# Seven products for a unit pair of the first MLP layer in chunks 3 to 6, and four operand transposes moved into the attention stage

## The chip, the cores and the metric

The kernel runs on one core of a Trainium2 chip. The metric is the device time of one execution in microseconds (us). All times below are us unless marked ns. TensorE (PE) multiplies matrices, VectorE (DVE) and ScalarE (ACT) do elementwise work, GpSimd (POOL) masks, scales and issues loads, SyncE (SP) issues loads and stores. Each engine works through its own queue in order.

## The reference

Forgetting attention, and behind it a two-layer MLP with a tanh gelu. Inputs are float32.

```python
scores = scale * np.matmul(q, k.transpose(0, 1, 3, 2))      # 8 batches, 8 heads, 576 tokens, head size 64
cum = np.cumsum(np.log(np.clip(f, 0.0001, 1.0)), axis=-1)
scores = np.where(causal, -1000000000.0, scores + cum[:, :, :, None] - cum[:, :, None, :])
attn = softmax(scores)                                      # over the keys
x = np.matmul(attn, v).transpose(0, 2, 1, 3).reshape(4608, 512)
out = gelu_tanh(x @ w_in) @ w_out                           # 512 -> 2048 -> 512
```

## The kernel before

The MLP works on chunks of 512 tokens (nine, numbered 0 to 8), the attention on groups of four heads of one batch (sixteen "quads"). xT holds x transposed, in four blocks of 128 features. A stage of the steady part has two halves: the MLP's first layer of chunk c, and then attention for two quads, with the second layer of chunk c woven into it as filler for TensorE. The order is written out by hand: TABLES[c] is a string of words, which play(c) turns into instructions; every engine gets its instructions in the order of the words. FRONT does the same for chunks 0 and 1. The words that matter here:

- Y and X load ScalarE's table for gelu and exp. O.512 puts out what is left of the last chunk's second layer. F.n and f.n put out n steps of this chunk's.
- P.k is a plain unit of the first layer (mlp_in, L369, L376): eight matmuls for 256 of the 2048 hidden features, and one gelu. With a third number, P.k.1, it takes its PSUM tile from the pool psO ("po", one buffer, otherwise used by the attention products) and not from psS ("s", two buffers, otherwise used by the scores).
- R.k, said three times, does the units k and k + 4 together by seven products of half the size in place of eight (seven_in, L417, L423, L428, L432). Product one goes to bank pa, two to pb (both in psS), three to pc and four to pd (both in psM, "m", two buffers, otherwise the banks of the second layer), product five to pa again; the second R puts one more on pc and the third one on pd. VectorE makes six operations of it: a copy of pa, and adds from PSUM, three of which fill output tiles (h_st, in the pool ostage, three buffers, otherwise the tiles of the output stores). They are 28 matmuls of 256 columns against 16 of 512.
- R needs sums of weights, K.k.n (w_sums, L405: four operations on VectorE; they overwrite a part of w_in, so P.k and P.k+4 can't be used after them, and store three sums in an old chunk's part of xT, HOMES), and sums of x, T (x_sums, L390: four operations on VectorE for chunk c + 1, stored in chunk c's part of xT).
- G makes the sums that the second layer's own seven products need (gelu_sums, L483 to L489).
- TK.i and TQ.i transpose the loaded k and q of a quad on VectorE (L193), LK.i and LQ.i load those of a quad (L187, GpSimd's queue), LV loads v of a batch (L164, SP's queue). Buffers of k and q alternate between even and odd quads.
- S.i.r are scores and exp (L256, L264), M.i.r masks on GpSimd (L270, called selects below), D.i the denominators (L343 to L347), V.i.x an attention product and its xT product on VectorE (L355), VW.i the scaled v on GpSimd (L210, "vw product"), CL.i a small copy on VectorE (L215) that waits for VW.i.
- The second layer's output adds (L529) are VectorE's, its stores (L517) SP's. Its two banks are freed by the last output adds.

In stage c, the quads are q2 = 2c + 2, q3 = 2c + 3, q4 = 2c + 4. Before the change, R is used in chunks 7 and 8 alone. Chunks 2 to 6 are eight P each, with all of TK, TQ, LK and LQ for the next two quads near the start of the MLP half. K.1.0 to K.1.2 stand in the MLP of chunk 3, K.3.0 to K.3.2 in that of chunk 4, and K.1.3, K.3.3 and T at the end of stage 6.

Of the kernel before, what the change touches and what calls it, by code (L numbers as in the profile page):

```python
# [16 lines left out]
def kernel(  # L17
# [53 lines left out]
    """  # L71

    FRONT = """
        TQ.0 B.2.256 TK.1 SB TR LP.2@LQ.0 B.2.128 CW S.0.0 B.5.384 B.1.256 Z TQ.1 vw.0.0 S.0.2 WI.0 LQ.2 M.0.0 B.3.384 H.1.0.1
        LP.3 B.1.256 vw.1.0 WI.1@LU.4 W H.1.1.1 WI.3 B.2.256 WI.2 H.1.0.0 M.1.0.1 D.0.0 M.1.0.0 H.0.1.1 V.0.0.0 H.0.1.0 B.2.256 M.0.1 H.1.1.0 V.0.1.0
        D.1.0 H.0.3.0 B.2.128 V.1.0.0 LX.1.1 H.0.3.1 V.1.1.0 m.0.3.2 H.1.3.0 m.0.3.4 B.1.256 VW.1.1 H.1.3.1 B.4.128 vw.0.1 D.0.1 M.1.3 S.1.2 M.1.1 LK.2
        V.0.1.1 V.0.0.1 WO.0 J.0.1 D.1.1 J.0.0 WO.1@LV.1.1 V.1.1.1 V.1.0.1 J.0.3 WO.2@WI.1 VW.3 J.1.0 WO.3 LK.3 LQ.3 J.1.1 TQ.2 J.1.3 LQ.4
        LX.1.0@WO.2 TK.2 J.0.2 J.1.2 X LK.4 F.0.6 TK.3 B.3.256 S.2.0 LK.5 F.0.9 S.2.2 F.0.10 S.2.1 TQ.3 TQ.4 F.0.10 LV.2.0@LK.5 m.2.1 vw.2
        TK.4 S.3.0 f.0.1 M.2.2 CL.2 LQ.5 M.2.0 D.2 f.0.6 S.3.1 m.3.0 F.0.6 V.2.0 S.3.2 TK.5 LK.6 M.3.2 f.0.7 V.2.1 CL.3
        S.4.1 m.3.1 LQ.6 F.0.6 TQ.5 H.4.2.1 D.3 H.4.0.1 LQ.7 VW.4 H.4.0.0 V.3.1 v.3.0 f.0.3 H.4.2.0 CL.4 I.1.0 m.4.1 U.0 LV.2.1@LQ.5 I.1.4  # L80
        TQ.6 m.4.2.3 I.1.1 I.1.5 U.1 LV.3.0@LQ.7 m.4.2.2 TK.6 G.0 M.4.0 I.1.2 I.1.3 U.3 I.1.6 I.1.7 G.1.1.2 U.2 X F.1.14 S.5.0 f.1.28 S.5.1 D.4 M.5.0 f.1.16
# [2 lines left out]
    """

    HOMES = {1: 0, 3: 1}
    TABLES = {}
    TABLES.update(dict.fromkeys((2, 5), """
        Y O.512 P.0 P.1 TK.q3 TQ.q3 LK.q5 LQ.q5 TK.q4 TQ.q4 LK.q6 LQ.q6 LV P.4 P.5 G.0 P.2 P.3 P.6 P.7 G.1.1.2 X F.10 S.q3.0
        D.q2 M.q3.0 f.22 S.q3.1 V.q2.0 M.q3.1 VW.q3 f.18 S.q3.2 V.q2.1 M.q3.2 CL.q3 f.16 S.q4.0 D.q3 M.q4.0 f.18 S.q4.1 V.q3.0  # L90
        M.q4.1 VW.q4 f.9 V.q3.1 f.7 S.q4.2 M.q4.2 CL.q4
    """))
    TABLES.update(dict.fromkeys((3,), """
        Y O.512 P.0 P.1 TK.q3 TQ.q3 LK.q5 LQ.q5 TK.q4 TQ.q4 LK.q6 LQ.q6 LV K.1.0 K.1.1 K.1.2 P.4 P.5 G.0 P.2 P.3 P.6 P.7 G.1.1.2
        X F.10 S.q3.0 D.q2 M.q3.0 f.22 S.q3.1 V.q2.0 M.q3.1 VW.q3 f.18 S.q3.2 V.q2.1 M.q3.2 CL.q3 f.16 S.q4.0 D.q3 M.q4.0 f.18
        S.q4.1 V.q3.0 M.q4.1 VW.q4 f.9 V.q3.1 f.7 S.q4.2 M.q4.2 CL.q4
    """))
    TABLES.update(dict.fromkeys((4,), """
        Y O.512 P.0 P.1 TK.q3 TQ.q3 LK.q5 LQ.q5 TK.q4 TQ.q4 LK.q6 LQ.q6 LV K.3.0 K.3.1 K.3.2 P.4 P.5 G.0 P.2 P.3 P.6 P.7 G.1.1.2
        X F.10 S.q3.0 D.q2 M.q3.0 f.22 S.q3.1 V.q2.0 M.q3.1 VW.q3 f.18 S.q3.2 V.q2.1 M.q3.2 CL.q3 f.16 S.q4.0 D.q3 M.q4.0 f.18  # L100
        S.q4.1 V.q3.0 M.q4.1 VW.q4 f.9 V.q3.1 f.7 S.q4.2 M.q4.2 CL.q4
    """))
    TABLES.update(dict.fromkeys((6,), """
        Y O.512 P.0 P.1 TK.q3 TQ.q3 LK.q5 LQ.q5 LV P.4 P.5 G.0 P.2 P.3 P.6 P.7 G.1.1.2 X F.10 S.q3.0 D.q2 M.q3.0 f.22 S.q3.1
        V.q2.0 M.q3.1 VW.q3 f.18 S.q3.2 V.q2.1 M.q3.2 CL.q3 f.16 D.q3 f.18 V.q3.0 v.q3.1 T K.1.3 K.3.3 f.18
    """))
    TABLES.update(dict.fromkeys((7,), """
        Y O.512 P.0.1 R.1 P.4.1 R.1 R.1 R.3 P.2.1 R.3 G.0.1.2 P.6 R.3 G.0.3.4 G.1.1.2 T
    """))
    TABLES.update(dict.fromkeys((8,), """  # L110
        O.512 P.0.1 R.1 P.4.1 R.1 R.1 R.3 P.2.1 R.3 G.0.1.2 P.6 R.3 G.0.3.4 G.1.1.2
    """))

    singles = ctx.enter_context(tc.tile_pool(name="singles", bufs=1))
    ostage_pool = ctx.enter_context(tc.tile_pool(name="ostage", bufs=3))
# [664 lines left out]
```

## Time and profile before

| | |
|---|---|
| median of three runs | 330.25 us (330.21 to 332.17) |
| profiled execution, span from first to last instruction | 328.4 us |
| around it (median less span) | 1.85 us |
| granted TensorE clock | 1.000 of full speed |
| matmul L369 (plain units of the first layer) | 448, 99.0 us busy |
| matmul L504 (second layer by seven products) | some 2100 in three groups, 94 us busy |
| VectorE transposes L193 | 32, 39.9 us busy |

The page does not list the profiled execution's own device time apart from its span; the 1.85 us between the span and the median is taken as what lies around it. A row of the timeline has: start, duration, engine, line, operation, output and inputs, shapes, count, and in brackets the idle time before it with what ended it. Rows of the chain of waits have start, duration and the work. TensorE is busy 96% of the span; that share counts matmuls that overlap in the pipeline, so the chain of waits is what tells whether it is at its bound.

### The profile page before, as it was taken

Reading aid. Unit: us, or ns where it says so; the run is one execution under the profiler, and the core shown is the slowest. Engines: PE = TensorE matmul, PEld = TensorE weight load, DVE = VectorE, ACT = ScalarE, POOL = GpSimd, SP = SyncE. Lnnn points to the kernel's source line nnn. Section 1 sums busy time; section 2 is a strip of 40 time slices with the busy share of each in tenths; the row PEclk is TensorE's granted clock in tenths of the full one; section 3 lists DMA queues with packets and bytes.
Section 4 is the critical chain, followed back from the end, with each engine's and each line's share of the span. In section 5 each row is a group of like instructions: output and inputs, shape, how many; then the busy total and the mean of one; then the engine's idle time right before and its main releaser. Section 6 shows DMA issues by size and latency. Waiting matters only on the chain.

```text
span 328.4 us, 11961 instructions
## 1 busy us (share of the span) xinstructions
PE 316.9 (96%) x5421; PEld 206.5 (63%) x5421; DVE 206.4 (63%) x323; ACT 201.7 (61%) x231; POOL 110.6 (34%) x155
## 2 busy tenths in 40 slices
PE   3999999999999999999999999999999999999995
PEld 1458844545776477646774577557754777787684
DVE  4686039884887865674567456636553767875772
ACT  4685576866767586668656775768675841721630
POOL 8985572510504415520544054303440140000000
PEclk9999999999999999999999999999999999999999
DMA  7999999861124990295129711761110102002012
GB/s 123 210 214 215 168 230 199 167 165 24 36 40 94 236 208 31 94 187 108 37 68 182 140 37 36 160 122 36 36 66 0 36 21 81 2 32 98 0 35 96
DMA packets 44323, 33.42 MB, mean 102 GB/s; under 512 B 27488, under 2 KB 37856, under 8 KB 44272
## 3 DMA queue, kind: packets, MB, share of 16 engines
q0 software_dynamic: 8848, 16.58, 28.0%
q1 hardware_dynamic: 35280, 16.01, 18.4%
q8 instruction: 42, 0.69, 0.9%
q14 instruction: 9, 0.07, 0.1%
q10 hardware_dynamic: 144, 0.07, 0.1%
HBM read 36.85 MB, written 9.44 MB: 141 GB/s over the span
## 4 chain that ended last, share of the span: by engine, by line
PE 86%; DMA 3%; DVE 3%; ACT 3%; POOL 2%; issue 2%; POOLq 0%; DVEq 0%; ACTq 0%
PE ps_h L369 29%; PE ps_w L504 25%; PE po L324 9%; PE ps_s L256 8%; PE pso L574 4%; PE ps_h L458 4%; DMA v_nat<-in_v_dram 2%; PE ps_cd L417 2%; ACT pt L264 2%; PE ps_ab L417 2%; PE po_m L310 1%; POOL vw L210 1%; DMA out_dram<-o_st 1%; POOL v_nat L164 0%; PE ps_o L324 0%
## 5 line engine op out<-in xcount | busy, mean ns | idle before, releaser
L264 ACT ACTIVATE pt<-ps_s 128x1024 bf16<-128x1024 f32 (+2 forms) x100 | 93.7, 988 | 39.4 <-PE ps_s L256 34.9
L369 PE MATMUL ps_h<-xT,w_in_sb 128*128 128x512 bf16 x448 | 99.0, 379 | 0.0
L376 ACT ACTIVATE gT<-ps_h 128x1024 bf16<-128x1024 f32 x56 | 57.2, 1022 | 49.9 <-PE ps_h L369 48.3
L270 POOL TENSOR_SCALAR_AFFINE_SELECT pt<-pt 128x512 bf16<-128x512 bf16 (+3 forms) x65 | 38.2, 597 | 132.9 <-ACT pt L264 131.8
L369 PEld LDWEIGHTS <-w_in_sb 128*128 128x128 bf16 x448 | 43.8, 98 | 50.1 <-issue 0.4
L504 PEld LDWEIGHTS <-gT 128*32 128x32 bf16 (+1 forms) x1253 | 50.9, 97 | 6.4 <-issue 1.7
L504 PE MATMUL ps_w<-w_out_sb,gT 128*32 128x256 bf16 (+1 forms) x1056 | 46.9, 273 | 0.0
L504 PEld LDWEIGHTS <-gsum 128*32 128x32 bf16 (+1 forms) x1256 | 38.9, 97 | 2.7 <-issue 1.4
L256 PE MATMUL ps_s<-qT,kT 32*128 32x64 bf16 (+5 forms) x896 | 36.8, 263 | 0.3 <-ACT pt L264 0.2
L483 DVE TENSOR_TENSOR gsum<-gT 128x1024 bf16<-128x1024 bf16 x16 | 11.0, 689 | 35.2 <-ACT gT L376 35.2
L504 PE MATMUL ps_w<-usum,gsum 128*32 128x256 bf16 (+1 forms) x832 | 30.7, 273 | 1.0 <-ACT snap L525 0.7
L355 DVE TENSOR_TENSOR xT<-po,rb 128x576 bf16<-128x576 f32 x26 | 19.6, 755 | 18.9 <-PE po L324 18.6
L193 DVE STREAM_TRANSPOSE kT<-k_c 128x576 f32<-128x576 f32 x16 | 20.0, 1247 | 17.8 <-DMA k_c<-in_k_dram 17.8
L210 POOL TENSOR_TENSOR vw<-v_nat,wT 128x1280 bf16<-128x1280 f32 (+1 forms) x13 | 30.4, 2338 | 0.1
L529 DVE TENSOR_TENSOR o_st<-ps_w,snap 128x512 f32<-128x512 f32 x31 | 21.3, 689 | 13.2 <-PE ps_w L504 11.8
L256 PEld LDWEIGHTS <-kT 32*128 32x128 bf16 x896 | 16.9, 93 | 17.4 <-issue 12.6
L324 PE MATMUL po<-pt,vw 128*32 128x64 bf16 (+4 forms) x624 | 22.5, 279 | 0.0
L324 PEld LDWEIGHTS <-vw 128*32 128x32 bf16 x672 | 14.3, 96 | 10.6 <-issue 3.7
L193 DVE STREAM_TRANSPOSE qT<-q_c 128x576 f32<-128x576 f32 x16 | 19.9, 1242 | 1.1 <-PE ps_s L256 0.5
L164 POOL DMA_DIRECT2D v_nat<-in_v_dram x20 | 15.3, 776 | 4.6 <-DMA w_out_sb<-in_moe_w_out_dram 4.6
L504 PE MATMUL ps_w<-usum,gT 128*128 128x256 bf16 (+1 forms) x197 | 16.4, 273 | 0.0
L574 PE MATMUL pso<-w_out_sb,gT 128*32 128x512 bf16 (+1 forms) x115 | 15.6, 380 | 0.0
(97 smaller groups left out, 327.0 us busy)
## 6 DMA issues: line engine op xcount, KB each, us to landing
out_dram<-o_st SPq DMA_DIRECT2D x35, 256.0 KB, 2.4
k_c<-in_k_dram POOLq DMA_DIRECT2D x16, 288.0 KB, 5.8
q_c<-in_q_dram POOLq DMA_DIRECT2D x16, 288.0 KB, 7.3
v_nat<-in_v_dram SPq DMA_DIRECT2D x16, 256.0 KB, 8.5
w_in_sb<-in_moe_w_in_dram POOLq DMA_DIRECT2D x4, 512.0 KB, 9.5
w_out_sb<-in_moe_w_out_dram POOLq DMA_DIRECT2D x4, 512.0 KB, 8.3
v_nat<-in_v_dram SPq DMA_DIRECT2D x16, 128.0 KB, 3.5
v_nat<-in_v_dram POOLq DMA_DIRECT2D x13, 128.0 KB, 6.9
```

The lines of the kernel that those rows point to most:

```text
L193: nc.vector.transpose(out=dst.rearrange("p s c -> p (s c)").bitcast(FP32) .rearrange("p (t a) -> p a t", a=S // 32), in_=src.rearrange("p ...
L210: eng.tensor_mul(vw[i % 2][:, t0:t1], vb[:, t0:t1, h0:h0 + 4, :], wT[:, i, t0:t1, :].unsqueeze(3).to_broadcast([128, t1 - t0, 4, D]))
L256: nc.tensor.matmul(tiles[h // 2][:, h % 2, c0:c0 + nq], key_columns(i, key, h, c), qq[32 * h:32 * h + 32, q0:q0 + nq, c], start=(c == 0 an ...
L264: nc.scalar.activation(p[:, 2 * g:2 * g + 2, off:off + n], t[:, :, 0:n], AF.Exp, scale=scale)
L270: nc.gpsimd.affine_select(out=x, in_=x, compare_op=ALU.is_ge, fill=0.0, base=0, pattern=pattern, channel_multiplier=-1)
L324: nc.tensor.matmul(po[r0:r0 + w.shape[-1], 448 + q0:448 + q0 + nq], w, p[:, h, col:col + nq], start=(key in (0, "low")), stop=(key in ("lo ...
L355: nc.vector.tensor_mul(xT[:, 2 * u + x, S * b + s0:S * b + s1], po, rbs[i, part])
L369: nc.tensor.matmul(ph[:, j, :], w_in_sb[:, dt, 128 * ft:128 * ft + 128], xT[:, dt, CH * c:CH * (c + 1)], start=(dt == 0), stop=(dt == N_DT ...
L376: nc.scalar.activation(gT[:, 2 * pr:2 * pr + 2, :], ph, AF.Gelu_apprx_tanh)
L504: nc.tensor.matmul(ps[c0:c0 + width, n, cols[0]:cols[1]], x[:, j, 128 * n + c0:128 * n + c0 + width], w[:, j, cols[0]:cols[1]], start=(fir ...
L529: nc.vector.tensor_add(st, ps, kept[name])
L574: nc.tensor.matmul(pso[c0:c0 + cols, :], gT[:, ft, 128 * n + c0:128 * n + c0 + cols], w_out_sb[:, ft, :], start=(ft == 0), stop=(ft == N_F ...
```

## The change

R.1 takes the place of P.1 and P.5 in chunk 3, and R.1 and R.3 that of P.1, P.5, P.3 and P.7 in chunks 4, 5 and 6. P.0 and P.4 (and P.2 in chunks 4 to 6) go to psO. For that, the weight sums K.1 move to the attention half of stage 2, K.3 to that of stage 3, and T stands at the end of stages 2 to 5 too. The transposes of k and q for the quads q4 and q5 move into attention, behind the first product of q2 and of q3; the loads for q6 go behind the masks M.q3.2, those for q7 to the end of the stage. In chunks 4 and 5, LV comes after the R.1 words. FRONT is wrapped otherwise, with the same words. Tables 7 and 8 have the same words.

```diff
-    TABLES.update(dict.fromkeys((2, 5), """
-        Y O.512 P.0 P.1 TK.q3 TQ.q3 LK.q5 LQ.q5 TK.q4 TQ.q4 LK.q6 LQ.q6 LV P.4 P.5 G.0 P.2 P.3 P.6 P.7 G.1.1.2 X F.10 S.q3.0
-        D.q2 M.q3.0 f.22 S.q3.1 V.q2.0 M.q3.1 VW.q3 f.18 S.q3.2 V.q2.1 M.q3.2 CL.q3 f.16 S.q4.0 D.q3 M.q4.0 f.18 S.q4.1 V.q3.0
-        M.q4.1 VW.q4 f.9 V.q3.1 f.7 S.q4.2 M.q4.2 CL.q4
-    """))
...
+    TABLES[2] = """
+        Y O.512 P.0 P.1 TK.q3 TQ.q3 LK.q5 LQ.q5 TK.q4 TQ.q4 LK.q6 LQ.q6 LV P.4 P.5 G.0 P.2 P.3 P.6 P.7 G.1.1.2 X F.10 S.q3.0 D.q2 M.q3.0 f.22 S.q3.1
+        V.q2.0 K.1.0 M.q3.1 VW.q3 f.18 S.q3.2 V.q2.1 K.1.1 M.q3.2 CL.q3 f.16 S.q4.0 D.q3 M.q4.0 f.18 S.q4.1 V.q3.0 K.1.2 K.1.3 M.q4.1 VW.q4 f.9 V.q3.1
+        f.7 S.q4.2 M.q4.2 CL.q4 T
+    """
+    TABLES[3] = """
+        Y O.512 P.0.1 R.1 P.4.1 R.1 R.1 TK.q3 TQ.q3 LK.q5 LQ.q5 LV P.2 G.0 P.3 P.6 P.7 G.1.1.2 X F.10 S.q3.0 D.q2 M.q3.0 f.22 S.q3.1 V.q2.0 TK.q4 TQ.q4
+        M.q3.1 VW.q3 f.18 S.q3.2 V.q2.1 K.3.0 M.q3.2 LK.q6 LQ.q6 CL.q3 f.16 S.q4.0 D.q3 M.q4.0 f.18 S.q4.1 V.q3.0 TK.q5 TQ.q5 M.q4.1 VW.q4 f.9 V.q3.1
+        K.3.1 f.7 K.3.2 K.3.3 S.q4.2 M.q4.2 CL.q4 T LK.q7 LQ.q7
+    """
+    TABLES[4] = """
+        Y O.512 P.0.1 R.1 P.4.1 R.1 R.1 LV R.3 P.2.1 R.3 G.0.1.2 P.6 R.3 G.0.3.4 G.1.1.2 X F.10 S.q3.0 D.q2 M.q3.0 f.22 S.q3.1 V.q2.0 TK.q4 TQ.q4
+        M.q3.1 VW.q3 f.18 S.q3.2 V.q2.1 M.q3.2 LK.q6 LQ.q6 CL.q3 f.16 S.q4.0 D.q3 M.q4.0 f.18 S.q4.1 V.q3.0 TK.q5 TQ.q5 M.q4.1 VW.q4 f.9 V.q3.1 f.7
+        S.q4.2 M.q4.2 CL.q4 T LK.q7 LQ.q7
+    """
...
+    TABLES[6] = """
+        Y O.512 P.0.1 R.1 P.4.1 R.1 R.1 LV R.3 P.2.1 R.3 G.0.1.2 P.6 R.3 G.0.3.4 G.1.1.2 X F.10 S.q3.0 D.q2 M.q3.0 f.22 S.q3.1 V.q2.0 M.q3.1 VW.q3 f.18
+        S.q3.2 V.q2.1 M.q3.2 CL.q3 f.16 D.q3 f.18 V.q3.0 v.q3.1 T f.18
+    """
```

Tables 3, 4 and 6 of before are as table 2, with the K words named above; table 6 also ends without quads 4 and later. TABLES[5] after is the same as TABLES[4].

More of the change, by code (lines that the diff above doesn't have):

```diff
@@ L73 @@
     FRONT = """
[L74 to L81, printed above, removed]
@@ L82 @@
-        S.5.2 V.4.0 m.5.2.3 f.1.10 VW.5 V.4.1 CL.5 m.5.2.2 LQ.8 S.6.0 f.1.10 M.5.1 D.5 f.1.7 S.6.1 V.5.1 f.1.12 V.5.0 vw.6 S.6.2
-        m.6.1 M.6.2.2 m.6.0 m.6.2.3 LK.7 LK.8 CL.6 LX.3.1@LK.6
+        TQ.0 B.2.256 TK.1 SB TR LP.2@LQ.0 B.2.128 CW S.0.0 B.5.384 B.1.256 Z TQ.1 vw.0.0 S.0.2 WI.0 LQ.2 M.0.0 B.3.384 H.1.0.1 LP.3 B.1.256 vw.1.0
+        WI.1@LU.4 W H.1.1.1 WI.3 B.2.256 WI.2 H.1.0.0 M.1.0.1 D.0.0 M.1.0.0 H.0.1.1 V.0.0.0 H.0.1.0 B.2.256 M.0.1 H.1.1.0 V.0.1.0 D.1.0 H.0.3.0 B.2.128
+        V.1.0.0 LX.1.1 H.0.3.1 V.1.1.0 m.0.3.2 H.1.3.0 m.0.3.4 B.1.256 VW.1.1 H.1.3.1 B.4.128 vw.0.1 D.0.1 M.1.3 S.1.2 M.1.1 LK.2 V.0.1.1 V.0.0.1 WO.0
@@ new lines @@
+        J.0.1 D.1.1 J.0.0 WO.1@LV.1.1 V.1.1.1 V.1.0.1 J.0.3 WO.2@WI.1 VW.3 J.1.0 WO.3 LK.3 LQ.3 J.1.1 TQ.2 J.1.3 LQ.4 LX.1.0@WO.2 TK.2 J.0.2 J.1.2 X
+        LK.4 F.0.6 TK.3 B.3.256 S.2.0 LK.5 F.0.9 S.2.2 F.0.10 S.2.1 TQ.3 TQ.4 F.0.10 LV.2.0@LK.5 m.2.1 vw.2 TK.4 S.3.0 f.0.1 M.2.2 CL.2 LQ.5 M.2.0 D.2
+        f.0.6 S.3.1 m.3.0 F.0.6 V.2.0 S.3.2 TK.5 LK.6 M.3.2 f.0.7 V.2.1 CL.3 S.4.1 m.3.1 LQ.6 F.0.6 TQ.5 H.4.2.1 D.3 H.4.0.1 LQ.7 VW.4 H.4.0.0 V.3.1
+        v.3.0 f.0.3 H.4.2.0 CL.4 I.1.0 m.4.1 U.0 LV.2.1@LQ.5 I.1.4 TQ.6 m.4.2.3 I.1.1 I.1.5 U.1 LV.3.0@LQ.7 m.4.2.2 TK.6 G.0 M.4.0 I.1.2 I.1.3 U.3
@@ L84 @@
+        I.1.6 I.1.7 G.1.1.2 U.2 X F.1.14 S.5.0 f.1.28 S.5.1 D.4 M.5.0 f.1.16 S.5.2 V.4.0 m.5.2.3 f.1.10 VW.5 V.4.1 CL.5 m.5.2.2 LQ.8 S.6.0 f.1.10 M.5.1
+        D.5 f.1.7 S.6.1 V.5.1 f.1.12 V.5.0 vw.6 S.6.2 m.6.1 M.6.2.2 m.6.0 m.6.2.3 LK.7 LK.8 CL.6 LX.3.1@LK.6
     """
@@ L87 @@
     TABLES = {}
-    TABLES.update(dict.fromkeys((2, 5), """
-        Y O.512 P.0 P.1 TK.q3 TQ.q3 LK.q5 LQ.q5 TK.q4 TQ.q4 LK.q6 LQ.q6 LV P.4 P.5 G.0 P.2 P.3 P.6 P.7 G.1.1.2 X F.10 S.q3.0
-        D.q2 M.q3.0 f.22 S.q3.1 V.q2.0 M.q3.1 VW.q3 f.18 S.q3.2 V.q2.1 M.q3.2 CL.q3 f.16 S.q4.0 D.q3 M.q4.0 f.18 S.q4.1 V.q3.0
-        M.q4.1 VW.q4 f.9 V.q3.1 f.7 S.q4.2 M.q4.2 CL.q4
-    """))
[L93 to L105, printed above, removed]
@@ L106 @@
-    """))
-    TABLES.update(dict.fromkeys((7,), """
+    TABLES[2] = """
[7 more added lines that the diff above has]
+        K.3.1 f.7 K.3.2 K.3.3 S.q4.2 M.q4.2 CL.q4 T LK.q7 LQ.q7
@@ new lines @@
+    """
[4 more added lines that the diff above has]
+    """
+    TABLES[5] = """
+        Y O.512 P.0.1 R.1 P.4.1 R.1 R.1 LV R.3 P.2.1 R.3 G.0.1.2 P.6 R.3 G.0.3.4 G.1.1.2 X F.10 S.q3.0 D.q2 M.q3.0 f.22 S.q3.1 V.q2.0 TK.q4 TQ.q4
+        M.q3.1 VW.q3 f.18 S.q3.2 V.q2.1 M.q3.2 LK.q6 LQ.q6 CL.q3 f.16 S.q4.0 D.q3 M.q4.0 f.18 S.q4.1 V.q3.0 TK.q5 TQ.q5 M.q4.1 VW.q4 f.9 V.q3.1 f.7
+        S.q4.2 M.q4.2 CL.q4 T LK.q7 LQ.q7
@@ L108 @@
+    """
+    TABLES[6] = """
+        Y O.512 P.0.1 R.1 P.4.1 R.1 R.1 LV R.3 P.2.1 R.3 G.0.1.2 P.6 R.3 G.0.3.4 G.1.1.2 X F.10 S.q3.0 D.q2 M.q3.0 f.22 S.q3.1 V.q2.0 M.q3.1 VW.q3 f.18
+        S.q3.2 V.q2.1 M.q3.2 CL.q3 f.16 D.q3 f.18 V.q3.0 v.q3.1 T f.18
+    """
+    TABLES[7] = """
         Y O.512 P.0.1 R.1 P.4.1 R.1 R.1 R.3 P.2.1 R.3 G.0.1.2 P.6 R.3 G.0.3.4 G.1.1.2 T
-    """))
-    TABLES.update(dict.fromkeys((8,), """
+    """
+    TABLES[8] = """
         O.512 P.0.1 R.1 P.4.1 R.1 R.1 R.3 P.2.1 R.3 G.0.1.2 P.6 R.3 G.0.3.4 G.1.1.2
-    """))
+    """
```

## The prediction

> **What bounds the kernel now.** First the page: parts 1 and 4 say that TensorE is the bound nearly everywhere.
>
> ```profile
> PE 316.9 (96%) x5421; PEld 206.5 (63%) x5421; DVE 206.4 (63%) x323; ACT 201.7 (61%) x231; POOL 110.6 (34%) x155
> PE 86%; DMA 3%; DVE 3%; ACT 3%; POOL 2%; issue 2%; POOLq 0%; DVEq 0%; ACTq 0%
> ```
>
> Second, the chain of waits in order of time: each chunk from 2 to 6 opens with eight plain units in one unbroken piece, and chunk 8, which has the seven-product units already, shows what the new form costs.
>
> ```profile
> 171.75 13.81 PE ps_h L369 x64
> 185.57 1.09 PE ps_w L504 x10
> ...
> 206.23 13.81 PE ps_h L369 x64
> ```
> ```profile
> 299.31 1.73 PE ps_h L369 x8
> 301.03 0.87 PE ps_ab L417 x8
> 301.90 0.87 PE ps_cd L417 x8
> 302.78 0.44 PE ps_ab L417 x4
> 303.21 1.73 PE ps_h L369 x8
> ...
> 312.32 8.73 PE ps_w L504 x80
> ```
>
> From one chunk's first unit to the next is 206.23 - 171.75 = 34.48 us, and TensorE waits for nothing in it. So every microsecond of matmul saved is saved for good, and every new wait of TensorE is lost for good. Third, the timeline at the turn from attention to MLP (chunk 3 into 4; the other turns repeat it), where the change puts new work on VectorE:
>
> ```profile
> 169.06 0.76 DVE L355 TENSOR_TENSOR xT<-po,rb 128x576 bf16<-128x576 f32 x1 [0.97 <-PE po L324]
> 169.25 2.33 POOL L210 TENSOR_TENSOR vw<-v_nat,wT 128x1280 bf16<-128x1280 f32 x1
> 169.73 0.68 DVE L529 TENSOR_TENSOR o_st<-ps_w,snap 128x512 f32<-128x512 f32 x1
> 171.61 0.22 DVE L215 COPY vw<-vw 64x256 bf16<-64x256 bf16 x1 [1.20 <-POOL vw L210]
> 171.86 0.69 DVE L529 TENSOR_TENSOR o_st<-ps_w,snap 128x512 f32<-128x512 f32 x1
> 172.39 1.28 ACT L228 ACT_TABLE_LOAD   x1
> 172.44 1.23 POOL L270 TENSOR_SCALAR_AFFINE_SELECT pt<-pt 128x512 bf16<-128x512 bf16 x2 [0.86 <-ACT pt L264]
> ```
>
> The last output add of the old chunk (171.86) stands behind the copy L215, and that behind GpSimd's vw product. Fourth, two places where VectorE works on two SBUF operands while GpSimd works:
>
> ```profile
> 86.64 2.71 POOL L210 TENSOR_TENSOR vw<-v_nat,wT 128x1280 bf16<-128x1280 f32 x1
> ```
> ```profile
> 87.06 2.82 DVE L489 TENSOR_TENSOR gsum<-gT,gsum 128x1024 bf16<-128x1024 bf16 x1
> ```
> ```profile
> 102.77 0.72 POOL L270 TENSOR_SCALAR_AFFINE_SELECT pt<-pt 128x512 bf16<-128x512 bf16 x1 [12.22 <-ACT pt L264]
> ```
> ```profile
> 102.91 0.85 DVE L299 TENSOR_TENSOR pt<-pt,causal 128x512 bf16<-128x512 bf16 x1
> ```
>
> L489 takes 0.69 elsewhere and ended only after the vw product; L299 takes 0.42 elsewhere. So GpSimd holds such a VectorE operation until it is through. The word transposes and the adds from PSUM show no such thing (a transpose at 32.38 beside a vw product: 1.26, as ever).
>
> **The change part by part.** *Matmuls.* Four plain units and two seven-product units of chunk 8 take 312.32 - 299.31 = 13.01; eight plain units 13.81. So a pair of units in the new form saves 0.40. The change has one such pair in chunk 3 and two in chunks 4, 5 and 6: seven, 7 x 0.40 = 2.8 us removed from the path.
>
> *Transposes into attention.* Starts 1.08 apart (172.47, 173.56, 174.64), so 2.16 a pair, off the path before and after. The even pair goes behind the first xT product (158.38 to 159.13); VectorE idles 1.70 before the next one at 160.83, which slips by 0.4 and ends near 161.9, while the next user of po is TensorE at 163.08: hidden. The odd pair goes behind the xT product at 167.33; the next one moves from 169.06 to 170.2 and ends at 170.95. The first unit now uses po and waits for that at 171.59: 0.6 to spare, and were that cover gone, each 0.1 more costs 0.1. The output add of 169.73 ends at 171.6, so the copy of 171.61 keeps its time.
>
> *Sums of x at the end of a stage ("T").* Four operations, 1.67 in the row at 271.13, between that copy and the last output add. They have two SBUF operands, and GpSimd's two selects start at 172.44, in their midst. By the row at 102.91 each select costs such an operation 0.43. T runs from 171.86 to 171.86 + 1.67 + 0.86 = 174.4, the last output add from 174.35 to 175.05. TensorE, counted from 171.59: unit 0 1.73, product one 0.44, product two 0.44 (its x sum is ready at 172.7), product three 0.44, and product four at 174.64 needs the PSUM bank that the last output add frees: 0.45 lost. The copy of product one follows the add (174.95 to 175.65), product five needs it at 175.55: 0.15 lost. So 0.6 in each of chunks 5 and 6; bounds 0 (selects cost nothing, T through at 173.5) and 1.3.
>
> *Weight sums.* Seven operations of unit 1's and unit 3's weights (0.42 each) leave the MLP of chunks 3 and 4 and the end of stage 6, where TensorE did not wait: no gain. Eight now stand in stages 2 and 3. In stage 2 two of them precede a select by a hair and push it and the vw product by 0.15: chunk 3 loses 0.7. In stage 3, K.3.1 stands behind the late xT product at 170.9, under the vw product (to 171.58): it ends at 171.85. Output add to 172.5, two more sums and the selects 0.84 + 0.86, copy 0.24: T starts at 174.4. Product two, due at 173.76, waits for its x sum until 175.3: 1.5. Product four, then due at 176.15, waits for the output add (176.0 to 176.7): 0.6. Product five 0.15. So 2.2 in chunk 4; bounds 1.0 and 3.0.
>
> *Loads.* All k and q loads stay on GpSimd's queue. The first moved pair is issued after the select of 162.08 to 163.31; two issues of 0.55 fit ahead of the next select at 165.26. The second pair is issued right after the selects at the turn, just ahead of the last output store on SP's queue; the v load follows that store on SP as before, and its user is 34 us away. The third output tile of R.1 takes the buffer of that store: due near 179.0, 3.95 after the store's issue, with 0.1 of slack. Stores took 2.1 with no load beside (issue at 135.96), 3.8 with loads after them (207.06) and 6.2 with two k loads issued 1.3 and 0.8 before (104.77).
>
> ```profile
> out_dram<-o_st SPq DMA_DIRECT2D x1, 256.0 KB, 6.2
> ```
>
> Bounds 0 and 2.1 a chunk, in chunks 4 and 5 (chunk 6 has no loads). The order is that of the 6.2 row and of two more with a k or q load ahead (47.39 and 51.35, 5.2 and 5.0); but v loads on GpSimd's queue stood beside all three or just before, and here there are none. I take 4.4, midway from 3.8 to 5.0: 0.4 each once the slack is used, 0.8 in all.
>
> [...]
>
> *End of an MLP stage.* In chunk 7 the last half of the gelu sums ends at 289.91, 3.5 after the next matmul at 286.43; in chunk 3, 2.7 (153.6, 150.92). The denominators move by 0.8, and po is next needed 5.66 after that matmul, they are done at 4.2. The last gelu pushes the exp table and the exps by 0.4, to 4.95; scores need that PSUM at 5.10. Both hidden, the second by 0.15 only.
>
> **Sum.** Saved 2.8; lost 0.7 + 2.2 + 0.6 + 0.6 + 0.8 = 4.9. The span goes from 328.4 to 330.5. The median is 330.25, 1.85 above the span, and I keep that: 332.3 us.
>
> **Rivals.** *A, as above:* 332.3, own range 331.2 to 333.5. *B, the gain shows (faster):* the place is T at the turn. If it is through before the last output add is missed, as in chunk 7 (T at 271.13, no wait after), only chunk 4's sums behind the vw product cost, 1.0 to 1.4, so 330.25 - 2.8 + 1.2 = 328.7. It decides when the add ends by 174.6 instead of 175.05: half of the selects' 0.86 would do. For it: only one row shows a select holding VectorE. Against: the selects lie right in T. *C, the store is late:* k and q loads ahead of it as at 104.77, the R.1 tile waits 2.1 in chunks 4 and 5, 4.2 for 0.8: 335.7; it decides over 3.95 from issue. For it: the rows of 5.2 (47.39) and 6.2. Against: 2.1 to 3.8 in the stages that change.
>
> **How the numbers follow.** Chances: A 0.45, B 0.25, C 0.24, others 0.06 (half below B: no wait at all gives 330.25 - 2.8 = 327.45; half above C). The range 328.4 to 335.4 goes from B's better half to C's price and leaves out some 0.16. A difference of 1% (3.3 us) is about what a measurement of this kernel tells from no change. Faster by over 1% needs 326.95, which the whole saving does not reach: 0.03. Slower means above 333.55: C and the top of A, 0.27. The rest, 0.70, is within.
>
> **What would show it.** Right: TensorE's first ps_cd matmuls of chunks 3 to 6 wait for DVE o_st, and in chunk 4 ps_ab waits for DVE xT; the chunk's MLP matmuls alone add to 13.0. T's rows take 2.1 or more where selects run, against 1.67. Wrong: T at 1.67 beside the selects (B); h_st waiting for DMA out_dram (C); waits for po or ps_s inside attention, which I cost at nothing, or denominators late enough to hold TensorE, would break the sum at another place.

## The result and the profile after

The changed kernel takes 333.58 us (median of 19 runs, 331.46 to 335.84); the kernel before, run beside it, 330.55 (19 runs, 329.84 to 334.41). The measured ratio is 1.0077, with a 95% interval of 1.0057 to 1.0098 (the two medians alone give 1.0092): slower, by less than 1%. The profiled execution took 334.32, its span 332.6 against 328.4. One profiled execution shown further on (the version with another store tile, span 334.0) was a disturbed one; only stretches of it with a granted clock of 1.00 are read.

Lines of the new kernel are four higher than before: L369 is now L373, L417 L421, L423 L427, L428 L432, L529 L533, L390 L394, L405 L409, L324 L328, L210 L214, L270 L274. Parts 1 and 4 of the page:

```profile
PE 314.6 (95%) x5485; PEld 214.4 (64%) x5505; DVE 241.4 (73%) x381; ACT 202.8 (61%) x245; POOL 111.8 (34%) x155
PE 79%; DVE 6%; POOL 5%; issue 4%; ACT 3%; DMA 2%; POOLq 0%; DVEq 0%; ACTq 0%
```

TensorE is busy 2.3 us less than before (the forecast was 2.8 of matmuls saved; experiment 4 measures it without waits), and its share of the chain that ended last has fallen from 86% to 79%: what was lost is waiting. Where, the table of windows tells, cut at the borders of the two halves of each stage (start and end, length, then busy time of PE, PEld, DVE, ACT and POOL; behind them granted clock, DMA share, GB/s). Before, chunk 3 into 4, MLP and attention by turns:

```profile
137.11:150.92 13.81, 13.81 (x66) 6.27 (x64) 9.06 (x13) 9.30 (x10) 3.41 (x6) 1.00 0.92 195
150.92:171.59 20.67, 20.67 (x639) 15.89 (x638) 11.96 (x19) 14.29 (x17) 9.25 (x10) 1.00 0.14 40
171.59:185.40 13.81, 13.81 (x66) 6.27 (x64) 9.10 (x13) 9.31 (x10) 3.41 (x6) 1.00 0.96 196
185.40:206.06 20.66, 20.66 (x639) 15.87 (x638) 11.96 (x19) 14.28 (x17) 9.25 (x10) 1.00 0.13 39
```

After, chunk 3 to the MLP half of chunk 6:

```profile
137.49:151.34 13.85, 13.62 (x76) 7.43 (x76) 11.89 (x18) 9.41 (x12) 2.67 (x4) 1.00 0.79 149
151.34:174.31 22.97, 20.85 (x639) 15.91 (x638) 17.89 (x28) 14.29 (x17) 10.39 (x12) 1.00 0.29 60
174.31:189.50 15.19, 13.54 (x88) 8.56 (x88) 11.63 (x19) 9.34 (x14) 2.49 (x4) 1.00 0.79 153
189.50:211.50 22.00, 20.87 (x641) 15.72 (x638) 19.25 (x31) 14.75 (x18) 10.33 (x12) 1.00 0.28 63
211.50:224.52 13.02, 12.91 (x89) 8.62 (x88) 9.72 (x16) 9.17 (x14) 2.31 (x4) 1.00 0.76 163
224.52:245.09 20.57, 20.57 (x641) 15.74 (x639) 17.94 (x27) 14.68 (x18) 9.25 (x10) 1.00 0.09 29
245.09:258.57 13.48, 13.23 (x88) 8.59 (x88) 11.67 (x19) 9.24 (x14) 1.56 (x2) 1.00 0.12 40
```

A half in which TensorE's busy time equals its length, at a clock of 1.00, loses nothing. The MLP halves of chunks 3 to 6 come to 55.5 us, against 55.3 before (13.81 or 13.82 each): what the seven products saved there, waits took back. But the larger loss is in the *attention* halves of stages 3 and 4: 22.97 - 20.67 = 2.3 and 22.00 - 20.66 = 1.3, together 3.6 us at a place where the forecast had put nothing. TensorE's waits from 137 to 250 us name the releasers:

```profile
PE po L328 <- issue: 2.1, 1, 2.1
PE ps_cd L421 <- DVE h_st L427: 1.5, 1, 1.5
PE ps_s L260 <- issue: 1.1, 1, 1.1
```

And the chain of waits, which in the kernel before went through chunk 4's first layer in one piece of 13.81, now reads:

```profile
168.67 0.72 PE po L328 x21
169.40 2.12 issue
171.51 0.23 PE po L328 x3
...
177.47 5.84 DMA out_dram<-o_st
183.41 0.70 DVE h_st L427
184.15 0.60 PE ps_cd L421 x4
...
208.26 0.48 PE ps_s L260 x11
208.74 1.13 issue
209.86 0.39 PE ps_s L260 x4
```

"issue" is time in which an engine waits for nothing that the profile shows. At 169.40 TensorE stops in the middle of one attention product (21 matmuls, 2.12 us of nothing, then the last 3), at 208.74 in the middle of one set of scores. The profile shows no semaphore that it waits for. What is missing there the DMA view suggests. In attention TensorE uses up instructions fast (640 matmuls in 20.7 us, each with a weight load), and the DMA view lists two queues of the kind "instruction": in the whole run q8 moves 43 packets of 16 KB, 0.70 MB, and q14 10 packets, 0.08 MB. Of the trace's 12,201 instructions 10,990 are TensorE's matmuls and weight loads, 90%, and q8 moves 90% of the two queues' bytes, so I take q8 for TensorE's (an estimate from these counts; the trace does not name the engine). Before, q8's packets start every 3.4 to 4.2 us in the busy part of stage 3's attention; after, one starts at 162.2 and the next at 169.1. Part 3 of the DMA view for the stretch 162.5 to 169.0 of the changed kernel has no line for them at all:

```profile
q0 software_dynamic: 278, 0.58, 56.2%
q1 hardware_dynamic: 149, 0.15, 6.7%
```

and the equally long stretch before it, 155.7 to 162.2, has two:

```profile
q1 hardware_dynamic: 272, 0.26, 12.3%
q8 instruction: 2, 0.03, 2.8%
```

q0 in the first of them is the moved pair of loads, LK.q6 and LQ.q6. (They stand in the tables of stages 3 to 5, but in stage 5 no quad is left to load, so stages 3 and 4 alone have them.) That gives theory **F**: the k and q loads, now inside attention, make the instruction loads of TensorE late, and it runs dry. Its rival **V**: the stops come from the rest of what was moved into attention, VectorE's work above all.

The steps that were forecast are visible too. Chunk 3, VectorE and GpSimd at the turn (start, duration, engine, line):

```profile
137.72 2.43 DVE L394 TENSOR_TENSOR xT<-xT 128x512 bf16<-128x512 bf16 x4
138.33 1.54 POOL L274 TENSOR_SCALAR_AFFINE_SELECT pt<-pt 128x512 bf16<-128x512 bf16 x2 [0.88 <-ACT pt L268]
140.07 0.68 DVE L533 TENSOR_TENSOR o_st<-ps_w,snap 128x512 f32<-128x512 f32 x1
```

The four sums of x take 2.43 beside the two selects, not 1.67, and the last output add follows at 140.07; TensorE's product four waits for it, 0.27 of the 0.44 that this half loses, and product five for the copy behind that add. And chunk 4, VectorE's adds of R.1:

```profile
180.89 0.69 DVE L427 TENSOR_TENSOR h_st<-ps_cd,h_st 128x512 f32<-128x512 f32 x1 [0.48 <-PE ps_cd L421]
183.41 0.69 DVE L427 TENSOR_TENSOR h_st<-ps_cd,h_st 128x512 f32<-128x512 f32 x1 [1.82 <-DMA out_dram<-o_st]
```

The third output tile of R.1 waits for the last output store, which was issued at 177.47, behind the k and q loads of 176.52 and 177.11, and landed 5.84 later.

### The profile page after: what moved, and what is told of

Same layout as the page of the kernel before. It is cut to its first block, busy times and chain, and to the rows that moved or that the text cites. A ratio compares the mean times of both kernels' runs of the same rounds, so it can differ in the third digit from the quotient of the medians.

```text
span 332.6 us, 12201 instructions
## 1 busy us (share of the span) xinstructions
PE 314.6 (95%) x5485; PEld 214.4 (64%) x5505; DVE 241.4 (73%) x381; ACT 202.8 (61%) x245; POOL 111.8 (34%) x155
## 4 chain that ended last, share of the span: by engine, by line
PE 79%; DVE 6%; POOL 5%; issue 4%; ACT 3%; DMA 2%; POOLq 0%; DVEq 0%; ACTq 0%
PE ps_w L508 23%; PE ps_h L373 20%; PE ps_s L260 8%; PE po L328 8%; PE ps_cd L421 5%; PE ps_h L462 4%; PE pso L578 4%; PE ps_ab L421 3%; DMA out_dram<-o_st 2%; POOL vw L214 2%; ACT pt L268 2%; DVE xT L394 2%; PE po_m L314 1%; DVE o_st L533 1%; PE idle_ps L239 1%
## 5 line engine op out<-in xcount | busy, mean ns | idle before, releaser
L274 POOL TENSOR_SCALAR_AFFINE_SELECT pt<-pt 128x512 bf16<-128x512 bf16 (+3 forms) x65 | 39.3, 614 | 133.6 <-ACT pt L268 132.6
L373 PE MATMUL ps_h<-xT,w_in_sb 128*128 128x512 bf16 x320 | 75.7, 379 | 0.8
L380 ACT ACTIVATE gT<-ps_h 128x1024 bf16<-128x1024 f32 x42 | 42.9, 1021 | 41.8 <-PE ps_h L373 41.4
L373 PEld LDWEIGHTS <-w_in_sb 128*128 128x128 bf16 x336 | 32.7, 98 | 34.6 <-issue 0.4
L427 DVE TENSOR_TENSOR h_st<-ps_cd,h_st 128x512 f32<-128x512 f32 x44 | 30.0, 690 | 11.6 <-PE ps_cd L421 6.7
L214 POOL TENSOR_TENSOR vw<-v_nat,wT 128x1280 bf16<-128x1280 f32 (+1 forms) x13 | 30.4, 2339 | 0.1
L533 DVE TENSOR_TENSOR o_st<-ps_w,snap 128x512 f32<-128x512 f32 x31 | 21.3, 687 | 10.9 <-PE ps_w L508 9.1
L328 PE MATMUL po<-pt,vw 128*32 128x64 bf16 (+4 forms) x624 | 22.7, 279 | 2.1 <-issue 2.1
L328 PEld LDWEIGHTS <-vw 128*32 128x32 bf16 x672 | 14.4, 96 | 12.9 <-issue 6.0
L421 PEld LDWEIGHTS <-w_in_sb 128*128 128x128 bf16 x176 | 17.2, 97 | 7.5 <-issue 3.2
L432 ACT ACTIVATE gT<-h_st 128x512 bf16<-128x512 f32 x33 | 18.9, 622 | 2.4 <-DVE h_st L427 2.4
```

The lines of the kernel that those rows point to most:

```text
L214: eng.tensor_mul(vw[i % 2][:, t0:t1], vb[:, t0:t1, h0:h0 + 4, :], wT[:, i, t0:t1, :].unsqueeze(3).to_broadcast([128, t1 - t0, 4, D]))
L274: nc.gpsimd.affine_select(out=x, in_=x, compare_op=ALU.is_ge, fill=0.0, base=0, pattern=pattern, channel_multiplier=-1)
L328: nc.tensor.matmul(po[r0:r0 + w.shape[-1], 448 + q0:448 + q0 + nq], w, p[:, h, col:col + nq], start=(key in (0, "low")), stop=(key in ("lo ...
L373: nc.tensor.matmul(ph[:, j, :], w_in_sb[:, dt, 128 * ft:128 * ft + 128], xT[:, dt, CH * c:CH * (c + 1)], start=(dt == 0), stop=(dt == N_DT ...
L380: nc.scalar.activation(gT[:, 2 * pr:2 * pr + 2, :], ph, AF.Gelu_apprx_tanh)
L421: nc.tensor.matmul(ps[:, j], w[:, dt, 128 * j:128 * j + 128], x[:, dt], start=(first and j == 0 and dt == 0), stop=(dt == 1), skip_group_c ...
```

## The experiments

All times beside the kernel before on the same chip (330.4 to 330.6 in each of four groups: 1 to 4, 5 to 8, 9 to 11, 12). Edits are shown on one table; the same words change in the tables of stages 3 to 5 unless it is said otherwise.

**1. The loads alone, out of attention.**

```diff
-  V.q2.1 M.q3.2 LK.q6 LQ.q6 CL.q3 f.16 ... CL.q4 T LK.q7 LQ.q7
+  V.q2.1 M.q3.2 CL.q3 f.16 ... CL.q4 T LK.q6 LQ.q6 LK.q7 LQ.q7
```

> The changed kernel, with the two loads LK.q6 and LQ.q6 of stages 3 and 4 taken out of the middle of attention and put at the end of the stage, ahead of LK.q7. Theory F: TensorE's stop in attention (2.1 us in stage 3, 1.1 in stage 4, laid to no engine by the profile) is its own instructions coming late behind these loads. Then the attention halves of stages 3 and 4 go from 22.97 and 21.99 back to between 20.6 and 21.1, and no wait of TensorE is laid to 'issue'. The last output store now has four loads ahead of it, and VectorE no longer has the stop to catch up in, so the MLP halves of chunks 4 and 5 grow, to 15 to 17.5 and 13.5 to 16; in all 330.5 to 335. Theory V: the stop comes from the transposes that now stand in attention (VectorE late with po). Then the attention halves stay at 22 to 23 and the time rises by what the store costs.

Measured: 340.65 us (338.88 to 342.68), ratio 1.0314 (1.0262 to 1.0367). The attention halves of stages 3 and 4 are back at 20.66 and 20.57, and no wait for issue is left, with all of VectorE's moved work still there: F holds, V falls. But the time was missed by far, because the MLP halves of chunks 4 and 5 grew to 20.64 and 18.35. TensorE's waits, 137 to 250 us:

```profile
PE ps_cd L421 <- DVE h_st L427: 6.7, 2, 3.6
PE ps_ab L421 <- DVE xT L394: 1.2, 1, 1.2
PE ps_cd L421 <- DVE o_st L533: 0.5, 2, 0.3
```

Now four loads, issued from 173.56 to 175.19, are ahead of the store of 176.02, which lands 7.9 later; h_st waits for it, TensorE 3.58 in chunk 4, and 3.16 in chunk 5. And the price does not end with the wait:

```profile
184.73 0.60 PE L421 MATMUL ps_cd<-xT,w_in_sb 128*128 128x256 bf16 x4 [3.58 <-DVE h_st L427]
185.33 0.60 PE L421 MATMUL ps_ab<-xT,w_in_sb 128*128 128x256 bf16 x4
185.76 3.22 PE L373 MATMUL ps_h<-xT,w_in_sb 128*128 128x512 bf16 x8
```

```profile
178.00:185.00 7.00, 3.42 (x28) 2.54 (x27) 2.58 (x5) 2.35 (x4) 0.00 (x0) 1.00 1.07 216
185.00:191.70 6.70, 6.70 (x32) 3.31 (x30) 4.14 (x7) 3.28 (x6) 0.00 (x0) 0.75 0.44 89
```

Eight plain matmuls take 3.22 instead of 1.89, and the granted clock of the 6.7 us behind the wait is 0.75. Behind the wait of 3.16 it is 0.76 over 6.8 us. Behind the changed kernel's stop of 2.12 it stayed 1.00. The waits for xT and o_st are the forecast's step on the weight sums: with no stop in stage 3 to let VectorE catch up, it shows.

**2. The same loads into attention, in the kernel before.** Nothing else of the change is in.

```diff
-  TK.q4 TQ.q4 LK.q6 LQ.q6 LV ... M.q3.2 CL.q3 f.16 S.q4.0
+  TK.q4 TQ.q4 LV ... M.q3.2 LK.q6 LQ.q6 CL.q3 f.16 S.q4.0
```

> The kernel before, with one thing changed: LK.q6 and LQ.q6 of chunks 2, 3 and 4 moved from the MLP half to behind the masks M.q3.2 in attention. Transposes, plain units and sums stay where they were. Theory F: two or three of the three attention halves grow by 1 to 2.5 us each with TensorE waiting for nothing that the profile shows, and the time is 332 to 336. Theory V: nothing of VectorE's has moved, so the time stays within 0.3% of before (329.5 to 331.5).

Measured: 331.94 (331.11 to 332.26), ratio 1.0042 (1.0025 to 1.0059). The pairs are in stages 2, 3 and 4 there; one of the three stops TensorE, in stage 3:

```profile
PE ps_w L504 <- issue: 1.5, 1, 1.5
```

Instruction packets start at 162.1 and 168.7, 6.6 apart; in the two stages without a stop they are, from the second packet of the half on, at most 5.0 apart. The loads alone make the stop, without VectorE's moved work: V is refuted a second time. F's expectation was too high: not each pair of loads hits a packet.

**3. Another buffer for the third tile.** h_st takes a tile of the pool snap, whose tiles no store reads; the loads stay in attention.

```diff
-  gelu(1, 0, add(pd, u2, ostage_pool, "o"))
+  gelu(1, 0, add(pd, u2, snap_pool, "snap"))
```

> The changed kernel, with the third output tile of each seven-product unit pair (h_st of product seven) taken from the pool snap and not from ostage, so that it waits for no output store. If the store is what made it late (1.8 us of VectorE, 1.55 of TensorE in chunk 4), the MLP half of chunk 4 goes from 15.19 to 13.3 to 13.7 and the time falls by 1.0 to 1.8 us. If the store only stood for another delay, nothing changes by more than 0.5.

Measured: 331.59 (330.61 to 335.73), ratio 1.0041 (1.0021 to 1.0061), some 2.0 under the changed kernel; no wait for h_st. In the profiled execution stage 3 happened not to stop, and chunk 4's MLP half still takes 14.93 at full clock, now with the weight sums' waits. So the 13.3 to 13.7 that I expected was not reached: the store's wait is gone, but so is the stop in stage 3 that had covered the sums:

```profile
PE ps_ab L421 <- DVE xT L394: 1.1, 1, 1.1
PE ps_cd L421 <- DVE o_st L533: 0.3, 1, 0.3
```

**4. All three repairs.** The loads at the turn (1), the other tile (3), and the sums moved to where GpSimd is idle (but for the last K.3, which takes 0.63 beside a select): x sum 0 behind V.q2.1 and x sum 2 (word C, the same x_sums for the running chunk) behind the first R.1, so that two of four are left at the turn (T.0 and T.1.3 stand in the table of stage 2 too, C.2 in that of stage 6 too); three weight sums K.3 in the MLP of chunk 3, the fourth in its attention.

```diff
-  P.0.1 R.1 P.4.1 R.1 R.1 ... P.6 P.7 ... V.q2.1 K.3.0 M.q3.2 LK.q6 LQ.q6 CL.q3 f.16 S.q4.0 ... V.q3.1 K.3.1 f.7 K.3.2 K.3.3 ... CL.q4 T LK.q7 LQ.q7
+  P.0.1 R.1 C.2 P.4.1 R.1 R.1 ... P.6 K.3.0 K.3.1 K.3.2 P.7 ... V.q2.1 T.0 M.q3.2 CL.q3 f.16 K.3.3 S.q4.0 ... V.q3.1 f.7 ... CL.q4 T.1.3 LK.q6 LQ.q6 LK.q7 LQ.q7
```

> The changed kernel with all suspected costs taken away at once: loads of q6 at the end of the stage, the third tile from snap, the weight sums K.3 moved ahead (three into the MLP half of chunk 3, one behind f.16), and the sums of x split: the first behind V.q2.1, the second and fourth at the end of the stage, the third behind the first part of the next chunk's R.1. If the loads in attention, the store, K.3 behind the vw product and T beside the selects are the whole loss, the MLP halves of chunks 3 to 6 are 13.4, 13.0, 13.0, 13.0 (0.3 more each at most), attention 20.7, and the time is 2.3 to 2.9 us below before: 327.6 to 328.4. If the transposes in attention cost TensorE by themselves, it stays above 330.

Measured: 327.25 (326.95 to 327.65), ratio 0.9905 (0.989 to 0.992): 3.3 us under the kernel before, 6.3 under the changed one. From 137 to 250 us TensorE waits for nothing; the halves are what the matmuls alone take (chunks 5 and 6 13.02 as well):

```profile
137.01:150.43 13.42, 13.42 (x79) 7.44 (x76) 11.62 (x20) 9.40 (x12) 2.37 (x4) 1.00 0.81 154
150.43:171.09 20.66, 20.66 (x640) 15.88 (x639) 17.37 (x26) 14.28 (x17) 9.31 (x10) 1.00 0.13 37
171.09:184.11 13.02, 13.02 (x91) 8.60 (x89) 10.58 (x18) 9.24 (x14) 3.41 (x6) 1.00 0.93 194
```

So the 2.8 us of matmuls were there to be had. Experiments 5 to 8 take one repair back each.

**5. Without the loads' repair** (LK.q6 LQ.q6 behind M.q3.2 again).

> The version with all three repairs (327.25 us), but with the k and q loads of pair q6 back inside attention. F (the loads delay TensorE's instruction loads): TensorE stops with releaser issue, 1.0 to 2.1 us, inside attention of one to three of the stages 3 to 5, and never where the gap between two instruction loads stays under 5 us; time 328.3 to 332. N (the stops of the changed kernel came from late VectorE work, which the repairs have removed): no such stop, 327.0 to 327.6.

Measured: 328.97 (327.97 to 329.87), 1.7 over all three. Stops of 0.34 in stage 3 and 1.04 in stage 4, the gaps between instruction packets 5.3 and 6.2. F holds, N falls.

**6. Without the tile's repair** (the third tile from the output buffers again).

> The version with all three repairs (327.25 us), but with the third first-layer tile in the output buffers again, so that it waits for the last output store, which stands behind four k and q loads. C (order of the queue): the store takes 6.5 to 8 us, TensorE waits 2 to 3.6 us for DVE h_st in chunks 4 and 5 and the granted clock falls afterwards; 331 to 339. S (the store shares fairly with the loads): about 4 us, at most 0.5 lost a chunk, 327.3 to 328.3.

Measured: 327.80 (327.52 to 328.06), MLP halves of 13.42, 13.02, 13.02: no wait for h_st, so C as I put it fails. S is no better founded: the last output add is earlier by then, its store is issued at 173.54, *ahead* of the four loads (173.95 and after), and lands 2.4 later. The store's wait was a consequence of the late sums, and its price depends on which side of the loads it falls.

**7. Without the weight sums' repair** (K.3.0 behind V.q2.1, K.3.1 to K.3.3 behind V.q3.1).

> The version with all three repairs (327.25 us), but with the weight sums of unit 3 as the change put them: K.3.1 to K.3.3 behind the last xT product of stage 3. K (held under GpSimd's vw product and its selects): K.3.1 ends only with the vw product, the x sums and the copy of product one slip, TensorE waits for DVE xT in chunk 4; 1.0 to 2.5 lost in that chunk alone, 328.2 to 329.8. Rival (the sums run at their 0.42 each and are hidden): 327.0 to 327.6.

Measured: 329.03 (328.30 to 329.51), 1.8 over all three; chunk 4's MLP half 14.23, 1.21 lost. Rows of GpSimd, VectorE and TensorE at that turn:

```profile
169.37 2.33 POOL L214 TENSOR_TENSOR vw<-v_nat,wT 128x1280 bf16<-128x1280 f32 x1
170.30 0.74 DVE L359 TENSOR_TENSOR xT<-po,rb 128x576 bf16<-128x576 f32 x1
170.97 1.01 DVE L409 TENSOR_TENSOR xT<-xT,w_in_sb 128x512 bf16<-128x512 bf16 x1
...
174.76 0.61 PE L421 MATMUL ps_ab<-xT 128*128 128x256 bf16 x4 [0.73 <-DVE xT L394]
```

K.3.1 starts under the vw product and takes 1.01, not 0.42: it ends at 171.98, once that product is through (171.70). Product two then waits for its x sum, as forecast.

**8. Without the x sums' repair** (T whole at the end of the stage).

> The version with all three repairs (327.25 us), but with all four x sums at the end of the stage, beside GpSimd's two selects. T (each select holds a VectorE sum): the four take 2.1 to 2.5 instead of 1.67 and TensorE waits 0.3 to 0.7 for the last output add in each of chunks 3 to 6; 328.5 to 330. B (selects hold nothing): 1.67, no wait, 327.0 to 327.6.

Measured: 330.67 (329.29 to 333.09). The whole is less sharp than the halves: 13.84, 13.50, 13.50, 13.48 against 13.42, 13.02, 13.02, 13.02, so 0.42 to 0.48 lost in each of four chunks, 1.9 in all. Most of the rest of its profile's difference lies ahead of chunk 2, where the two kernels are the same: TensorE waits 1.50 there, until 25.51, for VectorE's vw, and the granted clock is 0.51 over the 3.45 us from 26.05. That the median is 3.4 over all three, and not 1.9, is not explained by this one profile. The row in chunk 3:

```profile
140.44 2.42 DVE L394 TENSOR_TENSOR xT<-xT 128x512 bf16<-128x512 bf16 x4
```

**9. Half the dose of F** (all three repairs, LK.q6 alone behind M.q3.2).

> The version with all three repairs (327.25 us), with only the k load of pair q6 inside attention, its q load at the turn. F (an instruction load of TensorE starts late while k and q loads are in flight): half the transfer, so gaps between instruction loads of at most 5 us and stops of 0 to 0.7 us; 327.2 to 328.5. Rival (any load that meets an instruction load costs the whole stop): 1.0 to 1.3 in one to three stages, 328.3 to 331.

Measured: 328.45 (326.89 to 331.64), too wide to tell by the time. Its profile: no wait for issue from 130 to 250 us, longest gap 5.2.

**10. Other traffic on another queue** (all three repairs, LV behind M.q3.2: five v loads on SP's queue inside attention, no k or q load).

```diff
-  P.4.1 R.1 R.1 LV R.3 ... V.q2.1 T.0 M.q3.2 CL.q3
+  P.4.1 R.1 R.1 R.3 ... V.q2.1 T.0 M.q3.2 LV CL.q3
```

> The version with all three repairs (327.25 us), with the v loads of each of stages 3 to 5 (SP's queue, four of 256 KB and a smaller one) moved from the MLP half into attention, and no k or q load there. F in general (any traffic that fills the 16 DMA engines delays instruction loads): gaps over 5 us and stops with releaser issue of 1 to 4 us a stage; 328.3 to 335. F for GpSimd's queue alone: no such stop. In both cases output stores of SP's queue stand behind the v loads, so waits for DVE o_st can come on top; they have another releaser.

Measured: 328.91 (328.40 to 329.49), 1.7 over all three. It has stops for issue, so it is not GpSimd's queue alone, but fewer than expected: 0.48 and 0.75, both in stage 4, behind two gaps of 5.0 in a row, for twice the bytes.

**11. The seven products without the move of the transposes** (all three repairs, but TK, TQ and their loads back in the MLP half).

```diff
-  P.0.1 R.1 C.2 P.4.1 R.1 R.1 LV R.3 ... V.q2.0 TK.q4 TQ.q4 M.q3.1 ... V.q3.0 TK.q5 TQ.q5 M.q4.1
+  P.0.1 R.1 C.2 P.4.1 R.1 R.1 TK.q3 TQ.q3 LK.q5 LQ.q5 TK.q4 TQ.q4 LK.q6 LQ.q6 LV R.3 ... V.q2.0 M.q3.1 ... V.q3.0 M.q4.1
```

> The version with all three repairs (327.25 us), with the transposes of the next pair (and their loads behind them) back in the MLP half, as before the change: the seven-product units without the move. In that half VectorE is busy 10.6 of 13.0 us already; four transposes of 1.08 make 14.9, so VectorE becomes its bound: 1.9 to 3.5 lost in each of chunks 4 and 5, 0 to 1 in chunk 3; 331 to 335.5, no stop with releaser issue. Rival (VectorE catches up in attention, where it idles 2 to 3 us): 327.0 to 328.

Measured: 343.67 (341.23 to 344.09), ratio 1.0389 (1.0352 to 1.0427); MLP halves of 20.0, 20.2 and 15.1 in chunks 4 to 6. Far over the expectation, which counted VectorE's busy time over the half. The four transposes come in one piece of 4.3 us ahead of the copy that frees a bank of R.3, so TensorE waits 4.12, in chunks 4 and 5 both, and then the clock is down again:

```profile
184.11 1.01 PE L421 MATMUL ps_ab<-xT,w_in_sb 128*128 128x256 bf16 x4 [4.12 <-DVE snap L436]
184.91 3.62 PE L373 MATMUL ps_h<-xT,w_in_sb 128*128 128x512 bf16 x8
```

```profile
184.00:191.59 7.59, 7.48 (x28) 3.57 (x28) 4.11 (x7) 3.01 (x5) 0.36 (x1) 0.63 0.66 115
```

So in this order, in one piece, the transposes can't stay in the MLP half beside the seven products. (Spread over that half they might cost less; that was not tried, so it is not shown that they had to leave it.)

**12. The sums' repair alone** on the changed kernel (loads in attention, tile in the output buffers).

> The changed kernel (333.58 us) with the sums of x and the weight sums moved alone; the third first-layer tile stays in the output buffers, the k and q loads of pair q6 stay inside attention. If the store waited only because late sums let the loads in ahead of it, the wait for DVE h_st goes too, and what is left is the stops with releaser issue, 1 to 2.1 us in one to three of stages 3 to 5: 328.5 to 332. If the store waits on its own account, 1.5 us more in chunk 4, with h_st waiting for DMA out_dram: 330 to 334.

Measured: 328.88 (328.16 to 330.37), ratio 0.996 (0.9934 to 0.9986), 4.7 under the changed kernel. No wait for h_st; one stop is left from 130 to 250 us, in stage 4:

```profile
PE ps_s L260 <- issue: 0.9, 1, 0.9
```

**The dose of F over all runs.** The longest gap between the starts of two instruction packets in an attention half (from its second packet on: the first gap begins in the MLP half, where TensorE uses few instructions, 66 to 91 matmuls a half against some 640 in attention), and the stop of TensorE at its end:

| version, stage | gap | stop |
|---|---|---|
| changed kernel, 3 | 6.9 | 2.12 |
| loads moved in the kernel before, 3 | 6.6 | 1.49 |
| another tile, 4 | 6.3 | 1.07 |
| sums alone, 4 | 6.3 | 0.95 |
| without the loads' repair, 4 | 6.2 | 1.04 |
| changed kernel, 4 | 6.1 | 1.13 |
| without the loads' repair, 3 | 5.3 | 0.34 |
| one load, 3 | 5.2 | 0 |
| another tile, 3 | 5.1 | 0 |
| v loads, 4 | 5.0 and 5.0, in a row | 0.48 and 0.75 |
| loads moved in the kernel before, 4 | 5.0 | 0 |
| sums alone, 3 | 4.7 | 0 |
| all three repairs, 3 and 4 (no k, q or v load in attention) | 4.0 | 0 |

The stop is the gap less about 5 (less 4.8 to 5.4 in these rows). The packets of an undisturbed half start some 3.7 us apart, so I estimate the margin at 1.3 us: a packet that is late by less costs nothing. The two gaps of the v loads fit only together: 10.1 less twice 3.7 less 1.3 is 1.4, against stops of 1.23.

Stage 2, whose loads nobody moved, has the same stop in small. Its k, q and v loads from the MLP half are still in flight when attention begins (GpSimd's queue q0 alone moves 0.60 MB from 117.5 to 124 us in the changed kernel), the first two packets there are 5.1 apart, and TensorE stops for 0.18:

```profile
125.50 0.38 PE L260 MATMUL ps_s<-qT,kT 32*128 32x320 bf16 x5 [0.18 <-issue]
```

In experiments 3, 5, 6 and 11 this stop is 0.34 to 0.51, behind gaps of 4.9 to 5.2; in the kernel before the gap is 4.9 and nothing stops. So experiment 6, with no load moved into attention, still has a stop of 0.51, outside the stretch from 137 us on that the other counts cover.

## Why the prediction was right and where it was not

The forecast held (332.3 against 333.58, within the range), but partly by luck: two errors nearly cancel. The MLP halves lost less than forecast, attention lost what had been costed at nothing. Waits in attention were among the forecast's own signs that its sum breaks at another place, and they came.

- *Matmuls*, 0.40 a pair: confirmed. With no wait the MLP halves take 13.42 and 13.02 (experiment 4).
- *Transposes into attention*, hidden: confirmed. In experiments 1 and 4 the attention halves with all of them are 20.57 to 20.66, as before; experiment 11 shows the price of not moving them.
- *Sums of x at the turn*, 0.7 in chunk 3 and 0.6 in chunks 5 and 6: the mechanism is right (2.43 for four, the last output add late), the size 0.44, 0 and 0.46. Chunk 5 lost nothing for a reason outside the step: the stop in stage 4's scores let VectorE get ahead, T (210.35 to 212.03) was through before the selects began at 212.28. The same in chunk 3 of experiment 8 gives 0.42. B's condition, that the selects hold nothing, is refuted; that each holds less than 0.43 is what the sizes say.
- *Weight sums*, 2.2 in chunk 4: right in mechanism, near in size where nothing covers it (1.9 in experiment 3 with T's share in it, 1.2 in experiment 7, where T is shorter). In the changed kernel it cost about 0.3, because TensorE had stopped for 2.12 just ahead, and K.3.1 ran behind the vw product instead of under it.
- *Loads, the last store*, 0.4 in each of chunks 4 and 5: under-sized in chunk 4 (5.84 to landing against my 4.4; TensorE's wait is 1.55 in the trace, and the half lost 1.9 by it), over-sized in chunk 5 (the store was issued at 212.66, ahead of the loads, and landed 2.4 later). Rival C put 2.1 on each of the two chunks: chunk 4 nearly paid it, chunk 5 paid nothing. Experiments 6 and 12 show what I had missed: the store's time hangs on whether it is issued ahead of the loads (2.4 there too), and that hangs on how late the sums make the last output add.

  The rows 5.84 and 7.9 with two and four loads ahead, against 2.4 with none, look like a store that waits for most of what is ahead of it. Theory S of experiment 6, a store that shares fairly with the loads, had put about 4 on it, some twice the 2.1 of a store with no load beside (an estimate); both rows with loads ahead are longer, and the one with four is longer than the one with two, so they speak against S here. What the DMA engines did in between was not traced further.
- *Loads, the moved pair*, at nothing: **this is the step that failed.** I counted the issues on GpSimd (two of 0.55 that "fit ahead of the next select") and asked who waits for GpSimd. I did not ask what the transfer itself collides with while it is in flight. By the experiments it delays the instruction loads: 3.6 us in the profiled execution, more than the whole net change of 2.1 that I forecast.
- *End of the MLP stage*, hidden: confirmed by the attention halves of experiment 4.

Added up, by the profiled executions: saved 2.8; lost in the MLP halves 0.44 + 2.17 + 0 + 0.46 = 3.1 (forecast 4.9), in the attention of stages 3 and 4 3.6 (forecast 0), and 0.2 in small differences elsewhere: 4.1 net, the difference of the spans (332.57 less 328.44), against a forecast of 2.1. The medians differ by 3.0; the number and length of the stops differ between runs (a pair of loads that stops TensorE in one kernel passes in another).

What stays open: the trace has no row for an engine that lacks instructions. That they were missing is inferred from the gaps, their proportion to the stops, and from moving the loads (experiments 1, 2, 5, 9, 10). Why some pairs of loads hit a packet and others don't (two of three in experiment 2 don't, nor does stage 3 in experiments 3 and 12) was not settled; nor was what a late packet waits for.
